# Sums of squares by column tiles in one more batch, with a newly searched order of the plan, in a fused attention and channel-mix kernel

## The chip, the cores and the metric

The kernel runs on one core of a Trainium2 chip. The metric is the device time in microseconds (us) of a whole execution. Every run of a changed kernel stands beside runs of the kernel before on the same chip, in rounds. A ratio is the mean time of one kernel's fast runs over that of the other's fast runs of the same rounds, so it is not quite the ratio of the medians that I quote beside it. A run is called slow when it lies over 1.5% above the fastest run of its kernel. The span of a profiled run is the time from its first to its last instruction. In the views, PE is TensorE, PEld its loading of weights, DVE VectorE, ACT ScalarE, POOL GpSimd and SP SyncE.

## The reference, cut to what matters

```python
kv  = einsum('bhsd,bhse->bhde', k, v)                  # 8 batches, 8 heads, 576 rows, 64 columns
out = einsum('bhsd,bhde->bhse', q, kv)
x   = out / sqrt(mean(out * out, -1) + 1e-6) * g_norm  # a sum of squares per row and head
x_prev = x shifted by one row
xk = mu_k * x + (1 - mu_k) * x_prev                    # xr the same with mu_r
k  = relu(xk @ w_k)                                    # 512 -> 1024
return sigmoid(xr @ w_r) * (k * k @ w_v)               # 1024 -> 512
```

## The kernel before

The attention works through batches 0 to 7, the channel mix through nine groups of 512 rows. Every piece of work has a name, and a list called ORDER gives the order in which the pieces are issued. Each engine executes its own pieces in that order, so a piece that waits holds up everything behind it on its engine. In the names, `q`, `k`, `v`, `u` and so on are followed by the batch or the group: `k4.2` is a product with w_k of group 4, `u6.00` an attention product of batch 6.

Three parts matter here. The first is the sum of squares. A full one multiplies by a 128-column matrix of ones and leaves the sums on all partitions. A compact one multiplies by 32 columns (`sel`), four head pairs at once, so that one inverse root suffices, and then has to spread the result over the partitions by way of DRAM:

```python
COMPACT = (5, 6, 7)
...
def ss_all(_):                                   # piece ss5: TensorE
    for i in range(2):
        for hp in range(NHP):
            nc.tensor.matmul(get(ps)[32 * hp:32 * hp + 32, i, 0:HS], sel, sq.t[:, hp, HS * i:HS * i + HS],
                             start=True, stop=True)
def rms_out(_):                                  # piece ro5: a small store, SyncE's queue
    nc.sync.dma_start(out=get(rd), in_=rc.t[0:128:16, :])
def rms_back(_):                                 # piece rb5: two broadcast loads, GpSimd's queue
    for e in range(2):
        nc.gpsimd.dma_start(out=get(rs)[64 * e:64 * e + 64],
                          in_=rd.t.rearrange("(i e) c -> e i c", e=2)[e].partition_broadcast(64))
```

The second is the way of q: from batch 3 on it is transposed by DMA from SyncE's queue, and a one-element copy on GpSimd (the gate) holds the next batch's loads back until the first transpose has landed.

```python
def q_turn(_, hs):                               # pieces qt6.0, qt6.2: SyncE's queue
    nc.sync.dma_start_transpose(out=get(qT)[:, hs].rearrange("q i (j p) -> q (i j) p", j=NJ),
                                in_=q2.t[:, hs].rearrange("p i j c -> p (i j c)"))
...
gate = add({"POOL": 0.3}, lambda _: nc.gpsimd.tensor_copy(out=turned, in_=qT.t[0:1, 0, 0:1]), ...)   # gate6
```

The third is the loads themselves: whole batches of q, k and v by GpSimd's queue, converted from fp32 to bf16 on the way, and the stores of the outputs by SyncE's queue.

## Time and profile before

| | before |
|---|---|
| median of 3 runs | 203.97 us |
| span of the profiled run | 201.7 us |
| TensorE busy | 192.6 us, 95% |
| VectorE busy | 147.2 us, 73% |
| DMA moved | 31.69 MB, 157 GB/s on average |

Each figure is a slice of 5.04 us: the busy share of TensorE and of the 16 DMA engines in tenths, and what the DMA engines moved.

```profile
PE   7999899999999999999999989999999999999991
DMA  6999999999969999999999949530742240003263
GB/s 173 200 202 207 204 205 205 204 203 248 171 100 200 217 217 193 173 207 216 207 251 248 203 70 231 156 104 5 185 143 51 66 132 15 2 0 101 69 193 108
```

TensorE has its 9s almost to the end.

### The profile page before, as it was taken

What the parts mean: (1) busy time and instruction counts of PE and PEld (TensorE: products, weight loads), DVE (VectorE), ACT (ScalarE), POOL (GpSimd) and SP (SyncE); (2) the same over time, 40 slices, a digit from 0 to 9 for tenths busy, and PEclk for the clock granted to TensorE, in tenths of its full rate; (3) what the DMA queues carried; (4) which work ended last, traced back from release to release, by engine and by line L of the source; (5) the groups of instructions that cost most, each with busy time, mean ns of one, the idle gap of its engine ahead of it and who ended that gap; (6) DMA issues with size and microseconds to landing.
All of it is one profiled execution on the core that took longest, in us unless ns stands there. A gap on an engine that the chain in (4) does not pass through costs nothing.

```text
span 201.7 us, 4116 instructions
## 1 busy us (share of the span) xinstructions
PE 192.6 (95%) x1629; PEld 103.4 (51%) x1651; DVE 147.2 (73%) x332; ACT 116.2 (58%) x148; POOL 33.4 (17%) x53
## 2 busy tenths in 40 slices
PE   7999899999999999999999989999999999999991
PEld 7867775454544454543457654444444444444451
DVE  1589988998898959799799985699486854432321
ACT  2588688666978597948723887268452226644020
POOL 7964314000050040040053010000200000000000
PEclk9999999999999999999999999999999999999998
DMA  6999999999969999999999949530742240003263
GB/s 173 200 202 207 204 205 205 204 203 248 171 100 200 217 217 193 173 207 216 207 251 248 203 70 231 156 104 5 185 143 51 66 132 15 2 0 101 69 193 108
DMA packets 39976, 31.69 MB, mean 157 GB/s; under 512 B 13812, under 2 KB 35092, under 8 KB 39956
## 3 DMA queue, kind: packets, MB, share of 16 engines
q0 software_dynamic: 21504, 18.11, 57.0%
q1 hardware_dynamic: 17780, 12.42, 25.9%
q10 hardware_dynamic: 672, 0.89, 1.3%
q8 instruction: 13, 0.21, 0.4%
q14 instruction: 7, 0.06, 0.1%
HBM read 35.33 MB, written 9.46 MB: 222 GB/s over the span
## 4 chain that ended last, share of the span: by engine, by line
PE 74%; DMA 13%; POOL 4%; ACT 3%; issue 2%; SPq 1%; DVE 0%; DVEq 0%; POOLq 0%; ACTq 0%
PE mm L795 25%; PE mm L875 24%; PE mm L853 12%; DMA w_k<-in_moe_w_k_dram 5%; DMA v<-in_v_dram 5%; DMA qT<-q 3%; PE at L649 2%; PE at L567 2%; PE mm L522 2%; PE mm L815 2%; PE mm L892 2%; PE at L892 2%; PE at L701 2%; POOL k L275 1%; POOL q L275 1%
## 5 line engine op out<-in xcount | busy, mean ns | idle before, releaser
L795 PE MATMUL mm<-xk,w_k 128*128 128x512 bf16 (+1 forms) x281 | 58.5, 355 | 0.4
L875 PE MATMUL mm<-w_v,sqk 128*128 128x512 bf16 x251 | 57.8, 379 | 0.6 <-issue 0.3
L799 ACT ACTIVATE relu<-mm 128x1024 bf16<-128x1024 f32 x36 | 36.9, 1024 | 27.1 <-PE mm L795 23.2
L795 PEld LDWEIGHTS <-w_k 128*128 128x128 bf16 x288 | 27.2, 98 | 26.7 <-issue 1.8
L875 PEld LDWEIGHTS <-sqk 128*128 128x128 bf16 x256 | 24.7, 98 | 29.2 <-issue 1.1
L853 PE MATMUL mm<-w_r,xr 128*128 128x512 bf16 x135 | 33.4, 379 | 0.8 <-issue 0.5
L879 DVE TENSOR_TENSOR out<-mm,sig 128x1024 f32<-128x1024 f32 x16 | 19.5, 1223 | 19.8 <-PE mm L875 15.8
L858 ACT ACTIVATE sig<-mm 128x1024 bf16<-128x1024 f32 x18 | 18.4, 1025 | 26.6 <-PE mm L853 26.5
L802 DVE TENSOR_TENSOR sqk<-relu 128x1024 bf16<-128x1024 bf16 x32 | 21.7, 687 | 10.9 <-ACT relu L799 10.7
L853 PEld LDWEIGHTS <-xr 128*128 128x128 bf16 x144 | 13.5, 98 | 15.6 <-issue 0.9
L185 ACT CAST uT<-at 128x576 bf16<-128x576 f32 x21 | 12.6, 641 | 12.2 <-PE at L649 12.2
L743 DVE TENSOR_SCALAR md<-d,cols 128x576 bf16<-128x576 bf16 x56 | 18.4, 371 | 0.3
L194 ACT ACT_TABLE_LOAD x12 | 15.4, 1283 | 0.2
L763 PE MATMUL mm<-zero 128*128 128x128 bf16 x137 | 12.3, 251 | 1.1 <-DVE zero L245 1.1
L717 DVE TENSOR_TENSOR xT<-uT,rs 128x1152 bf16<-128x1152 bf16 x14 | 10.5, 752 | 2.9 <-ACT rs L705 2.8
L656 DVE TENSOR_TENSOR sq<-uT 128x576 bf16<-128x576 bf16 x28 | 12.1, 451 | 0.8 <-ACT uT L185 0.6
L705 ACT ACTIVATE rs<-at,eps 128x576 bf16<-128x576 f32 x16 | 11.2, 738 | 1.8 <-PE at L701 1.7
L763 PEld LDWEIGHTS <-zero 128*128 128x128 bf16 x137 | 10.5, 116 | 2.9 <-issue 1.3
L684 POOL DMA_DIRECT2D rs<-rd x6 | 3.8, 634 | 44.2 <-DVE xk L746 20.6
L746 DVE TENSOR_TENSOR xk<-md,xT 128x1152 bf16<-128x1152 bf16 x14 | 10.6, 759 | 0.5
L746 DVE TENSOR_TENSOR xr<-md,xT 128x1152 bf16<-128x1152 bf16 x14 | 10.6, 759 | 0.5
L729 DVE TENSOR_TENSOR d<-xT 128x1152 bf16<-128x1152 bf16 x14 | 10.5, 753 | 0.2
(89 smaller groups left out, 175.2 us busy)
## 6 DMA issues: line engine op xcount, KB each, us to landing
out_dram<-out SPq DMA_DIRECT2D x22, 192.0 KB, 4.7
q<-in_q_dram POOLq DMA_DIRECT2D x6, 576.0 KB, 10.0
v<-in_v_dram POOLq DMA_DIRECT2D x6, 576.0 KB, 12.6
k<-in_k_dram POOLq DMA_DIRECT2D x6, 576.0 KB, 11.1
out_dram<-out SPq DMA_DIRECT2D x23, 128.0 KB, 2.2
rs<-rd POOLq DMA_DIRECT2D x6, 288.0 KB, 5.6
out_dram<-out SPq DMA_DIRECT2D x22, 64.0 KB, 6.6
w_k<-in_moe_w_k_dram POOLq DMA_DIRECT2D x2, 512.0 KB, 11.5
```

The lines of the kernel that those rows point to most:

```text
L185: nc.scalar.copy(out=dst, in_=src)
L194: nc.scalar.preload_act_table_set(name)
L743: nc.vector.tensor_scalar(out=get(md)[:, hp], in0=d.t[:, hp], scalar1=cols[:, m0 + hp:m0 + hp + 1], scalar2=None, op0=ALU.mult)
L746: nc.vector.tensor_tensor(out=dst[:, hs, c0:c0 + S], in0=md.t[:, hs], in1=xT.t[:, hs, 0:S], op=ALU.add)
L763: nc.tensor.matmul(get(k_ps[i])[:, 0, 0:128], zero[:, 0:128], zero[:, 128:256], start=not k_seen[i], stop=not k_seen[i])
L795: nc.tensor.matmul(get(ps)[:, fc % 2, a0:a1], w_k_sb[:, cc, 128 * fc:128 * fc + 128], xk[:, cc, x0:x0 + a1 - a0], start=(cc == 0), stop=(c ...
L799: nc.scalar.activation(out=get(rt), in_=ps.t, func=AF.Relu)
L802: nc.vector.tensor_mul(out=get(sqk)[:, 2 * f2:2 * f2 + 2, :], in0=rt.t, in1=rt.t)
L853: nc.tensor.matmul(get(ps)[:, ci % 2, :], xr[:, cc, n0:n0 + 128], w_r_sb[:, cc, :], start=(cc == 0), stop=(cc == NHP - 1))
L858: nc.scalar.activation(out=get(sg), in_=ps.t, func=AF.Sigmoid)
L875: nc.tensor.matmul(get(ps)[:, ci % 2, :], sqk.t[:, fc, 128 * ci:128 * ci + 128], w_v_sb[:, fc, :], start=(fc == 0), stop=(fc == NFC - 1))
L879: nc.vector.tensor_mul(out=get(ot)[:, xs, :], in0=ps.t[:, xs, :], in1=sg.t[:, xs, :])
```

## The change

Its intent: the compact sums, which are cheaper on TensorE and on ScalarE, in batch 4 as well, and an order searched anew so that the pieces fit. The diff has one line outside the list, and nearly the whole list is new. Its core, with cuts marked by dots:

```diff
-    COMPACT = (5, 6, 7)
+    COMPACT = (4, 5, 6, 7)
 ORDER, around batches 4 to 6:
-... ss4.10 ... ss4.00 ... rr4.10 ... ss4.11 ... rr4.00 rr4.11 mul4.2 ... ss4.01 rr4.01 mul4.0 ...
+... qt5.0 ss4 ... rr4 ro4 ... qt5.2 ... gate5 loadq6.0 ... rb4 mul4.0 mul4.2 d4.0 d4.2 ... loadk6.0 loadv6.0 ...
-... k4.4 qt6.0 qt6.2 ... u6.10 u6.01 ... rb5 mul5.0 ... u6.00 ... gate6 loadk7.0 ...
+... qt6.0 u6.00 ... u6.01 ... rb5 mul5.2 ... k4.4 k4.5 ... qt6.2 u6.11 u6.10 ... gate6 loadq7.0 ...
 ORDER, start:
-setup loadq0.2 ident ... w_k0 idle:3 k0.a0.1 ... w_k1 idle:6 k0.a1.3 ...
+setup loadq0.2 loadk0.2 loadv0.2 loadq0.6 ... ident ... w_k1 idle:8 k0.a1.2 ... w_k0 ... idle:3 k0.a0.2 ...
```

## The prediction

> **What bounds the kernel now.** I read the page first, then the chain that ended last, then TensorE's timeline and busy times by stretch, then the ScalarE and GpSimd timelines around the few waits. The busy line and the chain's shares:
>
> ```profile
> PE 192.6 (95%) x1629; PEld 103.4 (51%) x1651; DVE 147.2 (73%) x332; ACT 116.2 (58%) x148; POOL 33.4 (17%) x53
> PE 74%; DMA 13%; POOL 4%; ACT 3%; issue 2%; SPq 1%; DVE 0%; DVEq 0%; POOLq 0%; ACTq 0%
> ```
>
> 95% alone is no proof, since 137 fillers (L763, multiplications by zero) are in it. The chain, in order of time, tells what is real:
>
> ```profile
> 9.83 10.92 DMA w_k<-in_moe_w_k_dram
> 20.75 0.05 issue
> 20.80 1.49 PE mm L522 x12
> ...
> 95.52 0.39 PE at L671 x8
> ...
> 138.80 3.45 PE mm L875 x16
> ...
> 195.80 1.76 PE at L892 x16
> ```
>
> There are three parts. (1) Up to 20.80 us the channel mix waits for the first half of w_k: GpSimd issued it at 9.83, behind twelve q, k, v loads, and it landed at 20.75 while the queue moved 200 to 208 GB/s. (2) From 20.80 to 197.56 (195.80 + 1.76) TensorE works. The busy times by stretch leave about 2.5 us idle in those 176.8 (10.00 minus 9.75, 9.64, 9.95 ... in the ten-microsecond stretches). (3) From 197.56 to the span's end at 201.7 lie the last product, store and closing: 4.1 us. The measured time, 203.97, is 2.3 above the span.
>
> So in the middle only work taken off TensorE, or an idle gap closed, counts. The gaps I can name:
>
> ```profile
> 20.80 1.49 PE L522 MATMUL mm<-xk,w_k 128*128 128x256 bf16 x12 [0.59 <-DMA w_k<-in_moe_w_k_dram]
> ...
> 56.88 1.02 PE L875 MATMUL mm<-w_v,sqk 128*128 128x512 bf16 x4 [0.15 <-ACT sig L858]
> ...
> 116.46 0.95 PE L567 MATMUL at<-v,k 96*64 96x64 bf16 x48 [0.53 <-DMA v<-in_v_dram]
> ```
>
> The first lies in part 1; the other two are 0.68 us together. Most of the rest is pieces of 0.05 and 0.16 marked "issue", which any order will have.
>
> **What the Trainium skill says.** "TensorEngine Tiling (Array Packing)", section Tiling Modes: a 128x32 configuration has four column tiles that can work in parallel, and changing the mode drains the engine. The trace agrees on both: eight compact sums (sel, 32 columns) take 0.39 and 0.36 us in the chain, while two full ones (ones, 128 columns) take 0.24 to 0.25, so eight would take 0.98; the speedup is 2.6, not 4. "ScalarE: Activation LUTs", section What ACT_TABLE_LOAD costs, gives about 1283 ns for a load plus 1380 ns of drain. The trace has twelve L194 loads of 1283 ns, but no such drain: the load at 54.51 ends at 55.79 and the sigmoid starts at 55.81. I charge 1.28. "DMA: Bandwidth & Descriptors", section Issuing engines are not separate DMA queues, has it that loads from all queues share the same 16 engines; the flat 200 to 208 GB/s of the start fits. A new order of the same bytes therefore does not bring w_k much earlier.
>
> **The change part by part.** There are two parts.
>
> *Compact sums in batch 4.* Removed: four groups of two 128x288 multiplications by ones (4 x 0.245 = 0.98 us TensorE) and four inverse roots (4 x 738 ns = 2.95 us ScalarE). Added: eight by sel (0.37 us), one inverse root (740 ns), a small store and two broadcast loads (2 x 635 ns on GpSimd, 0.59 MB). TensorE saves **0.61 us**, which counts fully because it lies in part 2. ScalarE saves 2.2 us, which by itself counts nothing at 58%. Price: the way through DRAM. In batch 5 the sums start at 95.52, the root ends at 96.68, the loads go out at 101.83 after a wait for the small store and land about 5.6 later, so about 12 us in all. The new plan has batch 4's sums some 13 us of TensorE work (adding its pieces up) before batch 4's product on VectorE, and 24 before k4.4, the first reader. So it should be hidden, if barely on VectorE.
>
> *The new order.* Instruction counts per engine hardly change otherwise; fillers go from 137 to 132.
>
> Start: the twelve loads ahead of w_k are the same bytes, but the making of ident no longer stands behind the first GpSimd load (the second load went out at 2.39 after a start at 1.30 with 0.76 for the first). It moves after the fifth load. The early queue fills 0.3 to 0.4 us sooner, and as bandwidth limits, w_k should land sooner by about that: **-0.3**. The halves of w_k swap, which alone changes nothing. VectorE's work before the first xk is of the same size (13 to 14 us of durations in both). After the first w_k matmul only 3 fillers remain instead of 6 (each 0.057): **-0.17**.
>
> Middle: closing the two named gaps would give -0.68. I count half, **-0.3**, because the new order shortens leads elsewhere. Adding durations up to each reader on both engines: k2.6 comes 0.5 us of VectorE work after xk2.2, where the first k2 reader had 3 to 8; k3.6 has 0.9 after xk3.0 instead of 11; k5.6 has 0.9 after xk5.0 instead of 18. These leads overstate VectorE's need, since its instructions overlap by some 10% (durations add to 164 us, busy is 147), so most will just fit. The tightest ScalarE place is at about 94 to 105 us, before batch 6's u: a root (0.74), q relays moved from VectorE (1.02 + 1.02 + 0.83), sig3.0 (1.28 table + 1.03), **two table loads in a row** from the piece "table", which now stands between two sigmoids and so loads the root's set only to have it replaced (2 x 1.28), sig3.1 (1.03) and the kv copy (0.37): 9.9 us for 10 to 11 us of TensorE work. A late q load would show there as a TensorE wait. The total of table loads stays twelve plus the initial one, so without that stray piece it would have been ten. I allow **+0.5** for this and the short leads together, and **+0.2** at v0.2.1: it comes about 0.6 us earlier against the second half of w_v, which landed at 35.0.
>
> Tail: the last six multiplications' worth of pieces are the same and ordered the same, and the second r8 pair moves forward, which only permutes TensorE work: **0**.
>
> Sum: -0.61 - 0.3 - 0.17 - 0.3 + 0.5 + 0.2 = -0.7. A plan kept after a new search is more likely to fit its leads than my additions can tell, so I go to -1.1: **202.9 us**.
>
> **The rivals.**
>
> *A: nothing is lost in the new order.* All named gaps vanish and no new ones come: -0.61 - 0.4 - 0.17 - 0.68 = -1.9, so 202.1. For it: the order was searched. Against it: the old order was too, and leaves only 2.5 us. This also gives a floor: taking all 2.5 us would end at about 200.3, which a stream of "issue" pieces excludes. A gain above 2% (below 199.9) would need TensorE work to vanish that the diff does not remove, or w_k to land 3 us earlier at the same bandwidth.
>
> *B: the relay through DRAM and the in-order queues take the saving back.* Batch 4's broadcast load now stands in GpSimd's queue behind the gate that waits for batch 5's transposed q, and the small store stands behind those transposes in SyncE's queue. VectorE is in order too, so its product of batch 4 stops everything behind it, ksq and out included. For it, before:
>
> ```profile
> 101.83 1.26 POOL L684 DMA_DIRECT2D rs<-rd  x2 [10.89 <-DMA rd<-rc]
> 104.16 0.60 POOL L612 COPY turned<-qT 1x1 bf16<-1x1 bf16 x1 [1.07 <-DMA qT<-q]
> ```
>
> The broadcast and the gate do queue in one another's way there. Against: VectorE still had slack around that time (1.0 us idle before the product at 100.64). If it hits, TensorE waits 1 to 3 us between 95 and 115: 204 to 206.
>
> *C: the start gets worse.* VectorE is full from 15 to 25 us (4.96 to 5.00 of 5.00), so a badly placed piece delays the first xk directly. For it: that stretch was reordered most. Against it: xk0.2 and xk0.3 now come first and w_k1 needs just those. It would add 0.5 to 1: about 203.7.
>
> **Range and chances.** The certain gain is 0.6; start and gaps are worth at most 1.3 more, and new waits would cost 0 to 2. From A to a mild B gives 201.5 to 204.5. A gain over 2% needs 4.1 us, more than all idle time plus the saving: 4%. A loss over 2% needs several new waits at once: 2%.
>
> **What would show it.** Right: eight more short L671 and eight fewer L701 multiplications, L705 down from sixteen instructions to twelve; first L522 at about 20.4; two L194 next to each other near 100 us; TensorE busy 9.8 or more in all stretches from 30 to 190; the last multiplication ending near 196.5. Wrong: TensorE waits over 0.5 us put down to xk or uT between 55 and 120 (B), or a first L522 after 21 (C); a gain over 2 us would mean that I overlooked idle time inside TensorE's busy time.

## The result, and the profile after

The changed kernel took 212.65 us (median of 4 runs, 212.26 to 216.06) beside 204.18 of the kernel before. The ratio of the fast runs is 1.0417 (95% interval 1.0375 to 1.046): 4.2% slower, and far outside the predicted range.

The profiled run has a span of 210.5 us, 8.8 more than before. Its page has, of the parts shown of before, the busy line, the rows by slice (now 5.26 us each) and the granted clock:

```profile
PE 197.2 (94%) x1646; PEld 103.6 (49%) x1646; DVE 148.4 (70%) x328; ACT 115.1 (55%) x149; POOL 36.0 (17%) x55
...
PE   7979999999999999999674999999999999999992
...
PEclk9999999999999999999996699999999999999999
DMA  6999999999999999899999999334650006400445
```

TensorE's row has a hole, 6 7 4, between 100 and 116 us, and at its end and behind it two slices of low clock. The DMA row has its 9s as before, now up to 131 us, but for one 8. What TensorE waited for from 25 us on (columns: total us, times, longest):

```profile
PE at L649 <- DMA qT<-q: 4.2, 1, 4.2
PE mm L875 <- DVE out L879: 1.5, 1, 1.5
PE at L892 <- DVE out L899: 0.5, 1, 0.5
```

In the kernel before, the longest wait in that stretch was the 0.53 us for batch 6's v. The chain of what ended last shows the new one. First the stretch of the kernel before, then of the changed one (start, us, what):

```profile
98.66 0.03 issue
98.69 5.35 DMA qT<-q
104.04 0.02 issue
```

```profile
96.50 0.75 ACT rc L676
...
98.98 14.36 DMA qT<-q
113.33 0.04 issue
113.38 0.70 PE at L649 x8
```

Batch 6's first transpose goes out at nearly the same time in both (98.69 and 98.98). It lands after 5.35 us in one and after 14.36 in the other. Nothing stands ahead of it in SyncE's queue that was not there before; the transfer itself is slow. The last columns of the stretches from 100 to 115 us say how (columns: stretch, its length, busy time and count of TensorE, weight loads, VectorE, ScalarE, GpSimd, then granted clock, DMA busy share, GB/s), before and after:

```profile
100.00:105.00 5.00, 5.00 (x35) 2.22 (x35) 4.29 (x9) 1.23 (x2) 1.86 (x3) 1.00 1.28 256
105.00:110.00 5.00, 4.83 (x86) 3.77 (x80) 4.54 (x10) 1.53 (x2) 2.34 (x3) 1.00 1.02 244
110.00:115.00 5.00, 4.95 (x43) 3.34 (x43) 4.89 (x12) 3.51 (x6) 0.00 (x0) 1.00 1.31 202
```

```profile
100.00:105.00 5.00, 3.27 (x16) 1.34 (x14) 4.80 (x9) 4.96 (x7) 1.27 (x2) 1.00 1.26 222
105.00:110.00 5.00, 4.13 (x63) 2.10 (x62) 4.87 (x11) 1.57 (x3) 0.00 (x0) 1.00 1.17 134
110.00:115.00 5.00, 1.62 (x13) 0.91 (x13) 1.00 (x2) 1.12 (x2) 1.14 (x3) 0.72 1.25 91
```

The share is the time of all packets over the engines' time, so that one above 1 means that packets overlap on an engine. In the changed kernel the DMA engines are as busy, but from 105 us on they move only 134 and then 91 GB/s. The 244 and 202 before are mostly plain loads and stores and no fair comparison. The stretch in which the transposes ran before is one, 100 to 105 us: 256 GB/s at a share of 1.28.

The records of single packets in the two traces tell what ran beside what. Before, the 2304 packets of batch 6's two transposes (256 bytes each) ran from 101.7 to 104.5 us, 1017 of them in the microsecond from 103 in which they were alone, and batch 5's broadcast began with its packets at 104.4. In the changed kernel they ran from 103.1 to 117.5 us: 119 to 492 in each microsecond from 103 to 106, beside v's load, and 7 to 188 in each from 107 to 115, beside the broadcast (issued at 102.48, landed up to 14.7 us later). The broadcast's packets of 4608 bytes slowed as well, from 312 ns on average to 668.

What came between is on GpSimd's queue, before and after (start, us, engine, line, operation):

```profile
88.64 0.78 POOL L275 DMA_DIRECT2D q<-in_q_dram  x1 [1.08 <-ACT relu L799]
89.41 0.77 POOL L275 DMA_DIRECT2D k<-in_k_dram  x1
90.17 0.77 POOL L275 DMA_DIRECT2D v<-in_v_dram  x1
```

```profile
87.65 0.92 POOL L275 DMA_DIRECT2D q<-in_q_dram  x1 [1.08 <-DVE out L879]
88.56 1.27 POOL L684 DMA_DIRECT2D rs<-rd  x2
89.81 0.82 POOL L275 DMA_DIRECT2D k<-in_k_dram  x1
90.59 0.81 POOL L275 DMA_DIRECT2D v<-in_v_dram  x1
```

Batch 4's broadcast, `rs<-rd`, is the new line. With it k and v land at 103.0 and 107.2 instead of 99.2 and 102.8. Before, the last packet of v's load began 0.5 us after the transposes' first one; now the two run beside each other for 3.7 us, and so the transposes are still under way when the broadcast starts.

The last product ends at 206.97 instead of 197.56, 9.4 us later. Of that I can name: 1.0 by the first product of group 1 (43.32 against 42.30), 1.5 and 4.2 and 0.5 for the three waits, and about 2.4 for the 32 products of group 4 behind the long wait, which take 6.10 us at a low clock. Less 0.61 for the cheaper sums and 0.5 for the wait for v that is gone, this makes 8.5. About 1 us is spread over gaps that I do not name. Between the last product and the end of the span lie 3.5 us instead of 4.1.

### The profile page after: what moved, and what is told of

The parts are those of the page before. It is cut to its first block, busy times and chain, and to the rows that moved or that the text cites. A ratio compares the mean times of both kernels' runs of the same rounds, so it can differ in the third digit from the quotient of the medians.

```text
span 210.5 us, 4132 instructions
## 1 busy us (share of the span) xinstructions
PE 197.2 (94%) x1646; PEld 103.6 (49%) x1646; DVE 148.4 (70%) x328; ACT 115.1 (55%) x149; POOL 36.0 (17%) x55
## 4 chain that ended last, share of the span: by engine, by line
PE 84%; DMA 7%; DVE 5%; ACT 2%; SPq 1%; issue 0%; ACTq 0%
PE mm L795 28%; PE mm L875 23%; PE mm L853 14%; DMA qT<-q 7%; PE mm L763 3%; PE at L649 2%; PE at L567 2%; PE at L892 2%; PE mm L815 2%; PE mm L892 2%; PE at L701 1%; PE mm L522 1%; DVE xT L432 1%; PE at L627 1%; DVE xk L478 1%; PE at L671 1%
## 5 line engine op out<-in xcount | busy, mean ns | idle before, releaser
L795 PE MATMUL mm<-xk,w_k 128*128 128x512 bf16 (+1 forms) x288 | 61.6, 367 | 0.0
L875 PE MATMUL mm<-w_v,sqk 128*128 128x512 bf16 x256 | 58.4, 379 | 1.5 <-DVE out L879 1.5
L795 PEld LDWEIGHTS <-w_k 128*128 128x128 bf16 x288 | 28.4, 102 | 27.7 <-issue 2.0
L853 PE MATMUL mm<-w_r,xr 128*128 128x512 bf16 x144 | 34.3, 379 | 0.2 <-ACT sig L858 0.2
L879 DVE TENSOR_TENSOR out<-mm,sig 128x1024 f32<-128x1024 f32 x16 | 19.6, 1223 | 16.1 <-PE mm L875 10.6
L743 DVE TENSOR_SCALAR md<-d,cols 128x576 bf16<-128x576 bf16 x56 | 18.3, 369 | 0.3
L185 ACT CAST uT<-at 128x576 bf16<-128x576 f32 x18 | 11.0, 640 | 10.7 <-PE at L649 10.7
L194 ACT ACT_TABLE_LOAD x12 | 15.4, 1283 | 0.2
L763 PE MATMUL mm<-zero 128*128 128x128 bf16 x132 | 12.2, 255 | 1.1 <-DVE zero L245 1.1
L612 POOL COPY turned<-qT 1x1 bf16<-1x1 bf16 x4 | 2.4, 604 | 55.2 <-DMA qT<-q 55.2
L684 POOL DMA_DIRECT2D rs<-rd x8 | 5.0, 633 | 39.5 <-DMA rd<-rc 18.3
L763 PEld LDWEIGHTS <-zero 128*128 128x128 bf16 x132 | 10.4, 118 | 1.9 <-DVE zero L245 1.1
## 6 DMA issues: line engine op xcount, KB each, us to landing
v<-in_v_dram POOLq DMA_DIRECT2D x6, 576.0 KB, 14.9
k<-in_k_dram POOLq DMA_DIRECT2D x6, 576.0 KB, 12.4
```

What stands on the lines that cost most here:

```text
L194: nc.scalar.preload_act_table_set(name)
L743: nc.vector.tensor_scalar(out=get(md)[:, hp], in0=d.t[:, hp], scalar1=cols[:, m0 + hp:m0 + hp + 1], scalar2=None, op0=ALU.mult)
L763: nc.tensor.matmul(get(k_ps[i])[:, 0, 0:128], zero[:, 0:128], zero[:, 128:256], start=not k_seen[i], stop=not k_seen[i])
L795: nc.tensor.matmul(get(ps)[:, fc % 2, a0:a1], w_k_sb[:, cc, 128 * fc:128 * fc + 128], xk[:, cc, x0:x0 + a1 - a0], start=(cc == 0), stop=(c ...
L853: nc.tensor.matmul(get(ps)[:, ci % 2, :], xr[:, cc, n0:n0 + 128], w_r_sb[:, cc, :], start=(cc == 0), stop=(cc == NHP - 1))
L875: nc.tensor.matmul(get(ps)[:, ci % 2, :], sqk.t[:, fc, 128 * ci:128 * ci + 128], w_v_sb[:, fc, :], start=(fc == 0), stop=(fc == NFC - 1))
```

## The experiments

My theory after the traces was that the DMA engines are the cause: batch 4's broadcast, 0.59 MB where they are full, pushes the loads into the transposes and those into batch 5's broadcast. The rivals were the new order (its short leads, its start, its table loads) and the queues' order alone. Piece names are those of ORDER. All 18 kernels gave correct results. Where my theory forecast a loss, it was often larger than expected: e6, e9, e15 and e16 lie above their ranges, and so do e3, by 0.3 us, and e5, by 0.1.

### The waits of the changed kernel, one at a time

**e1_gate_first.** The gate that waits for batch 6's first transpose goes ahead of batch 5's broadcast on GpSimd, so that the two do not meet.

```diff
-... rb5 mul5.2 ... gate6 loadq7.0 ...
+... gate6 rb5 mul5.2 ... loadq7.0 ...
```

> Edit: in the changed kernel, GpSimd's gate of batch 6 (the tiny copy that waits for the first transposed q of batch 6) is moved ahead of batch 5's two broadcast loads, so these loads start only when that transpose has landed. Nothing else moves. Theory 1 (collision): the transpose of batch 6 took 14.4 us instead of 5.4 because it shared the DMA engines with batch 5's broadcast loads; then it should land by about 107 to 108 us, TensorE's 4.2 us wait before batch 6's u and the low clock after it (2.6 us) should go, and the time should fall from 212.4 to 205 to 207. Theory 2 (queueing: batch 6's k and v loads, pushed back by batch 4's extra 0.59 MB, hold the transpose up): the broadcast plays no part, the transpose still lands after 111 us, and the time stays above 211.

210.14 us, ratio 1.0318 (1.0274 to 1.0363). The transposes took 8.9 us, and TensorE waited for none. But the wait moved on to batch 5's x, whose broadcast now began at 109.0:

```profile
121.54 3.21 PE L795 MATMUL mm<-xk,w_k 128*128 128x512 bf16 x8 [2.38 <-DVE xk L746]
```

So keeping the two apart does quicken the transposes. Of the 9.0 us that the first one lost in the changed kernel, the meeting with the broadcast makes 5.5 by this run (14.4 against 8.9), and the rest, in which the loads ran beside it, 3.5 (8.9 against 5.35). The time was a miss, because the delay is passed on rather than removed.

**e2_u6_late.** Batch 6's first two attention products go behind four pieces of group 4, so that TensorE need not wait for the transpose.

```diff
-... qt6.0 u6.00 uc6.00 u6.01 uc6.01 rb5 ... k4.0 k4.1 relu4.0 qt6.2 ...
+... qt6.0 rb5 ... k4.0 k4.1 relu4.0 u6.00 uc6.00 u6.01 uc6.01 qt6.2 ...
```

> Edit: in the changed kernel, batch 6's first two u products (and their evictions) are placed behind four of group 4's k products instead of ahead of them. DMA is untouched. If what matters is only that TensorE's in-order queue has a late product at its head, the transpose still takes about 14 us, but TensorE works 3.45 us of it off: the wait should fall from 4.2 to about 0.8 us, the low clock should go, and the time should be 206 to 208. If another wait stands right behind it (a reader of batch 4's or 5's x), the time stays above 210.

212.92 us, ratio 1.0455: no gain, a miss. The first pair no longer waited, but the second transpose was late as well, and TensorE waited 4.4 us for that one. So the place of the waiting pieces alone is not the cause.

**e4_table_early.** The stray table load of ScalarE goes to the start, where the kernel before had it.

```diff
-... kv0.0 kvc0.0 ... ql6.3 ql6.2 table r3.2 ...
+... kv0.0 kvc0.0 table ... ql6.3 ql6.2 r3.2 ...
```

> Edit: the one stray load of the root's table is moved from between two sigmoids of group 3 to the start, into an idle stretch of ScalarE, as before. This removes the 1.28 us load that stands just ahead of the first inverse root at 12.44 us and one pair of loads at 102.6. Theory: the start of the changed kernel is bound by ScalarE and VectorE, not by w_k; the first k product, at 21.29 us, should start at 20.1 to 20.6 and the time fall by 0.6 to 1.3 us (211.1 to 211.8). The pair at 102.6 us should count nothing, as ScalarE then waits for TensorE. Rival (the pair delays batch 6): the wait of 4.2 us shrinks by 1 us or more and the time falls by over 2 us.

211.73 us, ratio 1.030 (1.0193 to 1.0407), with a widely spread set of runs and a profile that fell in the slow state. The first product with w_k began at 20.99 instead of 21.29, and the second lot of them at 22.60, behind VectorE's xk as before. That is less than the 20.1 to 20.6 expected. The transposes were still waited for, 5.4 us. So in this slow profile the first product came 0.3 us sooner, which by the next ones was gone, and the pair of loads in the middle is not the cause.

### The change taken apart

**e3_no_compact4** and **e5_order_alone.** The new order with full sums in batch 4. In e3 their pieces stand in one block, in e5 they are spread between products of group 2, and one output's eviction goes behind the last products.

```diff
-    COMPACT = (4, 5, 6, 7)
+    COMPACT = (5, 6, 7)
-... ss4 ... rr4 ro4 v2.2.0 v2.2.1 v2.3.0 v2.3.1 ... rb4 mul4.0 ...
+e5: ... ss4.00 rr4.00 v2.2.0 ss4.01 rr4.01 v2.2.1 ss4.10 rr4.10 v2.3.0 ss4.11 rr4.11 v2.3.1 ... mul4.0 ...
```

> Edit: the new order is kept, but batch 4's sums are full again (four full groups with four inverse roots where the compact one stood, no trip through DRAM). This adds 0.6 us to TensorE and takes 0.59 MB of broadcast away. Theory 2 (queueing): k and v of batch 6 land about 3 to 4 us earlier (v by about 104 instead of 107.2), the transpose follows, and the loss shrinks to under 3 us: 205 to 208. VectorE's 2.0 us wait for batch 4's factors and TensorE's 1.5 us wait for the output product should go in any case. Theory 1 alone (collision with batch 5's broadcast, which then would start right behind the earlier loads): the transpose still overlaps it and takes over 10 us; 209 to 212.

> Edit: the new order without the compact sums in batch 4, as in the last run, but the four full sums are spread between group 2's products so that TensorE doesn't wait 2.1 us for an inverse root (that wait was made by my placing them in a block), and the very last eviction is moved behind the products it held up (0.5 us). If the new order alone is sound and the trip through DRAM is what it cannot bear, this should be within 1.5 us of the kernel before: 203 to 205.5, with the transpose of batch 6 landing within 4 to 7 us and no TensorE wait over 1 us after 30 us. If the order itself loses much, it stays above 206.

e3 took 208.27 us (ratio 1.0205, 1.0133 to 1.0278, unclear), 2.3 us of it waits that my block of pieces made. e5 took 205.6 us, ratio 1.0083 (1.0041 to 1.0125). In both the first transpose of batch 6 landed in 3.9 to 6.4 us and TensorE waited for neither. The new order without the compact sums costs 0.8%, about 1.7 us; without the moved eviction, which removes a wait of 0.5 us, it might be a little more. In e5's profile the largest wait after the start is 1.5 us for an x of group 4.

**e6_compact_alone** and **e16_compact_clean.** The old order with compact sums in batch 4. In e6 the small store `ro4` stood ahead of batch 5's transposes, which made them land 2.4 us late (the gate behind them ran at 89.78 instead of 87.39), a fault that the changed kernel has not; e16 mends it.

```diff
-    COMPACT = (5, 6, 7)
+    COMPACT = (4, 5, 6, 7)
-... rr4.00 rr4.11 mul4.2 ... ksq3.0 ... qt5.2 ... ss5 loadq6.0 ... ss4.01 rr4.01 mul4.0 d4.0 ...
+e6:  ... ss4 rr4 ro4 ... qt5.0 gate5 ... qt5.2 ... ss5 loadq6.0 rb4 ... mul4.0 mul4.2 d4.0 d4.2 ...
+e16: ... ss4 rr4 ... qt5.0 gate5 ... qt5.2 ro4 ... ss5 loadq6.0 rb4 ... mul4.0 mul4.2 d4.0 d4.2 ...
```

> Edit: the old order with batch 4's sums compact, nothing else: sums, root and small store where the third full sum stood, the broadcast behind batch 6's q load (where the new order has it), batch 4's products, differences and the first mix moved together behind it. Theory: the 0.59 MB ahead of k and v of batch 6 push these back by 3 to 4 us (v lands at about 106 instead of 102.8), the transposes of batch 6 then share the engines with them and with batch 5's broadcast and take 9 us or more instead of 5.4. In the old order TensorE has 3.5 us of work between the landing and its use, so it waits less: 205 to 209. Rival (the trip is hidden in the old order and only the new order exposes it): 203.2 to 203.8, i.e. the 0.6 us of TensorE work saved.

> Old order, batch 4 compact, with its small store to DRAM behind batch 5's second transpose instead of ahead of the first (the run of the old order with batch 4 compact had it ahead, which sent batch 5's transposes out 2.4 us later). Theory 1 (0.59 MB more where the DMA engines are full): batch 5's transposes go out as in the kernel before, but k and v of batch 6 still land about 3 us later, and batch 6's transposes still meet batch 5's broadcast: 208 to 211.5. Rival (the small store's place in SyncE's queue was the cause in that run): 203.5 to 205.

e6 took 211.51 us (ratio 1.0381, 1.034 to 1.0422), e16 213.54 (1.0446, 1.0399 to 1.0493). The fault was not the cause; without it the time was no better. The chain and TensorE's timeline of e16:

```profile
100.42 14.26 DMA qT<-q
...
114.72 0.69 PE L648 MATMUL at<-qT,kv 64*64 64x288 bf16 x8 [5.88 <-DMA qT<-q]
```

That is the wait of the changed kernel, in the old order (which needs the second of batch 6's two transposes first, the new order the first). The compact sums of batch 4, with the pieces of batch 4 that move behind them, bring the whole loss by themselves: 4.5% here and 0.8% for the order in e5, against 4.2% for both together, so the two do not add up.

### The traffic alone

These four are the kernel before, full sums in batch 4 and all, with a load added whose result nobody reads. The broadcast ones copy the form and size of `rb4` (0.59 MB).

```diff
 e9:  ... ss5 loadq6.0
+     dum                                  # two broadcast loads
      ql6.2 ...
 e8:  ... loadk6.0 loadv6.0
+     dum                                  # the same, behind v
 e13: ... ss5 loadq6.0
+     dum                                  # nc.gpsimd.dma_start(out=dum, in_=part("q", 0, 0, H - 1)): plain, 0.52 MB
 e10: ... mul6.0 qt7.2
+     dum                                  # two broadcast loads, at 122.8 us
```

> Edit: the same two additional loads, but issued right behind q of batch 6 and ahead of its k and v, which is where the changed kernel has batch 4's broadcast. Theory: k and v of batch 6 land 3 to 4 us later (103 and 106), and batch 5's own broadcast, which stands behind them, meets the transposes: these take 9 us or more though nothing of the new order is here. If so, the time rises to 205 to 209 as in the run with the compact sums alone. If the transposes stay under 7 us, the place in the queue isn't what matters.

> Edit: the old kernel with two additional broadcast loads of the same form (64 partitions x 4 rows of 576, from a DRAM tile of zeros to a tile that nobody reads), issued right behind v of batch 6, so that they run while batch 6's q is transposed. All else is as before; v of batch 6 should land at 102.8 as before. Collision theory: the transposes take 9 to 14 us instead of 5.4, and each 256 B packet about 0.1 instead of 0.02 engine-us. Rival (only bandwidth counts): 0.59 MB at 200 GB/s is 3 us, so 5.4 becomes at most 8 us.

> The kernel before with one plain dummy load between batch 6's q and k loads, where the dummy broadcast stood: seven of the eight heads of batch 0's q again (0.52 MB written, packets of the size of the other q, k and v loads). Theory 1 (room on the DMA engines is what is short): as bad as the broadcast there, 210 to 216, v landing over 15 us after its issue. Theory 2 (it is the broadcast's form, packets of 4608 bytes that hold up the transposes' packets of 256): under 206, transposes in under 7 us.

> The kernel before with the same two dummy broadcast loads (0.59 MB) as in the two runs before, but issued behind batch 7's second transpose, at about 125 to 135 us, where the DMA share of the kernel before falls from over 0.9 to 0.2. Theory 1 (the DMA engines are full until about 116 us, and anything added there pushes back what stands behind it): within 0.5% of before, 203.5 to 205.0, and the dummy loads land in under 7 us. Theory 2 (broadcast loads cost by themselves, wherever they stand, by GpSimd's issuing or by disturbing VectorE): 207 to 213 as at the earlier places.

The awaited transpose is the second of batch 6, as in e16.

| run | median, us | ratio (95%) | awaited transpose, us | TensorE waited for it, us |
|---|---|---|---|---|
| e9, broadcast ahead of k and v | 215.76 | 1.0574 (1.0525 to 1.0623) | 17.8 | 7.4 |
| e8, broadcast behind v | 211.98 | none | 16.1 | 9.2 |
| e13, plain load ahead of k and v | 215.12 | 1.0543 (1.0486 to 1.0601) | 17.0 | 8.6 |
| e10, broadcast at 122.8 us | 203.74 | 0.9987 (0.9957 to 1.0016) | 8.3 | 1.4 |

e8 fell three times in four above 210 us and once at 205.24, so by the rule three of its runs are slow, its profile too, and it gets no ratio; I build nothing on it. It also missed its expectation for v (15.3 us, not 12.6). The others are plain. The same broadcast costs 12.0 us at 89 us and nothing at 123 us, just before the DMA row falls (the added load landed in 7.4 us there; under 7 was expected). In e10 the second transpose took 8.3 us and TensorE waited 1.4 for it before the added load was even issued, so the old order by itself is not free of such waits. A plain load of the same weight, in the ordinary packets of the q, k and v loads, costs nearly as much, 10.8 us. So neither the sums, nor VectorE's wait for them, nor the form of the added load is needed: added bytes in the full stretch are enough. Two things stay in all of these runs: batch 5's own broadcast, and, in e9 and e13, the added load's place ahead of k and v in GpSimd's queue. e14 and e15 below take them away. In e13 a wait of 8.6 us stood where the kernel before had none:

```profile
117.76 0.69 PE L649 MATMUL at<-qT,kv 64*64 64x288 bf16 x8 [8.63 <-DMA qT<-q]
```

### Where the broadcasts stand

**e15_rb4_behind_v6** and **e14_four_not_five.** Both start from e16. e15 puts batch 4's broadcast behind k and v; e14 makes batch 5's sums full, so that only one broadcast runs before 110 us, as in the kernel before.

```diff
 e15:
-... ss5 loadq6.0 rb4 ... loadk6.0 loadv6.0 r3.2 ...
+... ss5 loadq6.0 loadk6.0 loadv6.0 rb4 ... r3.2 ...
 e14:
-    COMPACT = (4, 5, 6, 7)
+    COMPACT = (4, 6, 7)
-... ss5 ... rr5 ro5 store2.1 r3.1 ... sig3.0 v3.0.0 v3.0.1 v3.1.0 ... rb5 mul5.0 ...
+... ss5.00 rr5.00 ... store2.1 r3.1 ss5.01 rr5.01 ... v3.0.0 ss5.10 rr5.10 v3.0.1 ss5.11 rr5.11 sig3.0 v3.1.0 ... mul5.0 ...
```

> As the run with the small store mended, with batch 4's broadcast behind batch 6's k and v loads in GpSimd's queue, so that they no longer stand behind it. If the order of the loads is what costs: v lands in under 14 us and the time is 203.5 to 206. If it is room on the DMA engines: the v wait goes, but the broadcast lands about 10 us after its issue, batch 4's x comes late and TensorE waits for it or for the output of group 3 before it, 207 to 212.

> As the run with the small store mended, but batch 5 goes back to full sums: as much broadcast before 110 us as in the kernel before, only one batch earlier. If the meeting of batch 5's broadcast with batch 6's transposes is the main cost: the transposes land in under 7 us and the time is 203.5 to 206. If the delay of batch 6's k and v by the broadcast ahead of them is the main cost: TensorE still waits 2 to 4 us for v, 206 to 209.

e15 took 214.66 us, ratio 1.0546 (1.0494 to 1.0597). k and v no longer stood behind the broadcast, but v still took 15.8 us (12.6 before), and the broadcast took 16.18 us to land, VectorE stood before its product with it, and TensorE waited for an output behind that:

```profile
PE mm L874 <- DVE out L878: 10.2, 1, 10.2
```

So the queue's order decides who waits, not whether somebody does. e14 took 205.64 us, ratio 1.0075 (1.0039 to 1.0111): with one broadcast in that stretch the transposes were not waited for, although v needed 16.6 us behind the broadcast and TensorE waited 0.8 for it. The first transpose took 9.3 us (issued at 99.67, the gate behind it at 108.95), where under 7 was expected; that is close to e1's 8.9, again without a broadcast beside it. Another 2.5 us are waits for ScalarE, which I put down to my placing of the roots. What does not fit is the second broadcast.

### Room made elsewhere

Three output tiles of groups 2 and 3 (1.57 MB) are stored later, for which the output buffers go from three to four. In e11 and e12 all three go behind batch 7's first transpose, in e18 and e19 two of them behind its second. e12 and e18 have full sums in batch 4; e11 is e6 with this, e19 is e16 with it.

```diff
-        "out": (3, (128, 2, C), FP32),
+        "out": (4, (128, 2, C), FP32),
-... store2.1#2 store1.1#2 store2.0 store1.1 rr5 ro5 store2.1 ... store3.0#2 store2.0#2 ... qt7.0 store3.0 ... qt7.2 ...
+e11, e12: ... store1.1#2 store1.1 rr5 ro5 ... qt7.0 store2.1#2 store2.1 store2.0#2 store2.0 store3.0#2 store3.0 ... qt7.2 ...
+e18, e19: ... store1.1#2 store1.1 rr5 ro5 ... qt7.0 store2.1#2 store2.1 ... qt7.2 store2.0#2 store2.0 store3.0#2 store3.0 ...
```

> The kernel before with the same three output tiles' stores put off and four output buffers, nothing else. Theory 1: the wait of 0.53 us for batch 6's v goes, v lands in under 12 us, and the time is 203 to 204.5. Theory 2: no change, 204, v still at 12.6. If putting off stores makes a wait for an output buffer, TensorE or VectorE will show it near the last output of group 4 and the time will be 205 or more.

> The old order with batch 4 compact (which ran at 211.5), and with three output tiles' stores (of groups 2 and 3, 1.57 MB) put off from about 88 to 108 us until behind batch 7's first transpose, with four output buffers in place of three. Theory 1 (room on the DMA engines): the v wait of 3.7 us and the long transposes go, 203 to 206. Theory 2 (queue order: k and v of batch 6 simply stand behind the broadcast in GpSimd's queue, and stores go by another queue): 209.5 to 212.

> The kernel before with the stores of groups 2 and 3 put off as in the earlier run (206.5), but those of two of the three output tiles behind batch 7's second transpose instead of ahead of it, where they held it up by 3.2 us. If the wait of 3.2 us was all that was lost: TensorE has no wait over 0.5 us between 90 and 140, 202.5 to 203.8, a little faster than before. If another transfer meets the late stores: 204.5 or more.

> Batch 4 compact in the old order without the fault in SyncE's queue (213.5), and the late stores that gave 202.75 alone. If the stores' 1.57 MB were room enough for the 0.59 MB of the broadcast: 202 to 204.5. If what counts is that two broadcasts, the transposes and the loads of batch 6 meet between 98 and 112 us, and the stores taken away lay mostly before that: 208 to 213.

e12 took 206.5 us (ratio 1.0118): the wait for v went and TensorE was busy without a gap up to 130 us, as expected, but then it waited 3.2 us for batch 7's second transpose, which stood behind the late stores. e18 takes that away: 202.75 us, ratio 0.9943 (0.9915 to 0.997), 0.6% faster than the kernel before, a small gain but clear of the noise. In the stretch from 30 to 190 us TensorE was busy 157.64 of 160 us before, and here:

```profile
30.00:190.00 160.00, 159.06 (x1220) 76.56 (x1219) 122.24 (x245) 95.29 (x111) 16.86 (x25) 1.00 0.82 151
```

e11 took 217.5 us (ratio 1.0644), 6 us more than e6, and missed badly. It carries e6's fault and e12's, but e12's shows as a wait of 0.75 us only; the awaited transpose of batch 6 took 17.1 us and TensorE waited 6.4 for it. Why the late stores made e6 worse is not shown, and it speaks against room alone as the measure. e19, free of both faults, took 209.59 us (ratio 1.0266, 1.0209 to 1.0323) against 213.54 of e16. So the stores' room gives about 4 of the 9 us back, and not the rest: the awaited transpose still took 12.4 us. The stores taken away lay largely before the meeting, and the meeting of transposes and broadcast remains.

### The low clock

**e21_fillers_in_wait.** The changed kernel with 80 multiplications by zero ahead of `u6.00`, where TensorE waits for the transpose.

```diff
 def u_mm(_, gp=gp, cs=cs, ps=ps):
+    for _ in range(80 if b == 6 and gp == 0 and cs.start == 0 else 0):
+        nc.tensor.matmul(get(ps)[:, 0, 0:128], zero[:, 0:128], zero[:, 128:256], start=True, stop=True)
     for x in range(2):
```

> The changed kernel with 80 multiplications by zero (about 0.057 us each, 4.5 us) put ahead of batch 6's first attention product, where TensorE waits 4.2 us for the transpose. If the low granted clock comes from the idle wait: the clock in 110 to 120 us is 0.95 or more, the 32 products of group 4 behind it take 3.5 us instead of 6.1, and the time is 209.5 to 211. If it comes from something else: the products take 6 us all the same, and the time is 212 to 213.5.

212.76 us, ratio 1.0439: the time did not move, a miss. The mechanism did show. First the timeline of the changed kernel, then of this one:

```profile
114.00 6.10 PE L795 MATMUL mm<-xk,w_k 128*128 128x256 bf16 x32
```

```profile
110.13 4.63 PE L647 MATMUL at<-zero 128*128 128x128 bf16 x80
...
115.06 3.67 PE L797 MATMUL mm<-xk,w_k 128*128 128x256 bf16 x32
```

The granted clock was 1.00 in 110 to 120 us (in the changed kernel 0.50 from 112.2 to 119.0), and the same 32 products took 3.67 us instead of 6.10. In the profiled run TensorE was 1.2 us later than in the other before the wait (105.69 against 104.49 at the same products; 0.6 of it dates from the start, where this execution had a clock of 0.50 from 14.9 to 18.3 us and the other had not), and after the products it had a gap of 1.08 us that the profile puts down to nothing. So 2.4 us is what the low clock costs the products; what it costs the kernel this run leaves open.

## Why the prediction was wrong

The prediction said 202.9 us in a range of 201.5 to 204.5, and gave slower by over 2% a chance of 2 in 100. It was wrong in direction. By its own steps:

- **What bounds the kernel.** Right for TensorE, and incomplete: I quoted the 200 to 208 GB/s for the start only and never read the DMA row beyond it. The row has its 9s up to 116 us but for one slice. An estimate: the loads convert fp32 to bf16, and one that the profile counts as 576 KB reads 1152 KB (8 x 576 x 64 x 4 bytes), so 205 GB/s written is some 410 read, close to the 425 that the Trainium skill, "DMA: Bandwidth & Descriptors", section Measured (HBM→SBUF, 128 partitions, SWDGE, issued from GpSimd), gives as measured for a load of 16 MB. By this estimate there was hardly room; no run here shows the limit itself.
- **The compact sums save 0.61 us of TensorE.** Right as a term, and the sums take 0.36 to 0.39 us here too.
- **"So it should be hidden, if barely on VectorE."** This is the step that failed. I priced the way through DRAM as a latency against a lead, 12 us against 13, and counted the 0.59 MB as nothing. At the 205 GB/s of that stretch, 0.59 MB are 2.9 us of all DMA engines. k and v landed 3.8 and 4.4 us later, which is somewhat more. This laid the loads beside the transposes (3.5 of the 9.0 us, by e1) and the transposes beside batch 5's broadcast (the other 5.5), where the engines moved 91 to 134 GB/s. e16 shows that this term alone makes 4.5%; e9 and e13 that the traffic makes it without any sums; e10 that it is free at 123 us; e14 that one broadcast fits there and two do not. I had cited the skill's statement that all queues share the 16 engines, from the section Issuing engines are not separate DMA queues, and used it only for w_k. These runs agree with it: a load from GpSimd's queue delayed a transpose from SyncE's by 9 us.
- **The start, -0.3 and -0.17.** w_k's first half landed at about 20.1 instead of 20.75, sooner than predicted, although it was issued no earlier (9.89 against 9.83). But the first product with it began at 21.29 instead of 20.80, because VectorE's xk came later. This is rival C, with its sign (a first L522 after 21) and its size, 1.0 us by group 1. The fillers saved nothing visible (12.2 us against 12.3 of L763).
- **The gaps, -0.3, and the short leads, +0.5.** e5 puts the whole new order, start included, at 0.8%, about 1.7 us, where I had -0.07 for it (-0.3 - 0.17 - 0.3 + 0.5 + 0.2). The two table loads side by side did occur, at 102.61, and cost nothing that e4 could show.
- **The trust in a searched order, -0.4.** Not borne out: the search's plan is slower than the old one in e5 too.
- **Rival B.** It named the right part, the relay through DRAM, and the right place, 95 to 115 us, and its waits of 1 to 3 us were 4.2 and 1.5. But it looked for the fault in queues and in VectorE's order. Its sign, waits put down to xk or uT, did not come: TensorE waited for qT itself and for an output. Its counterargument, VectorE's slack, says nothing of the DMA engines. The low clock behind a long wait was in no rival. The Trainium skill has it: "TensorE: Matmul & The Clock Gate", Part 1, says that after an idle window of about 3.4 us the clock is halved, and comes back after as long a busy one. The trace agrees on the half: a wait of 4.2 us, and a granted clock of 0.50 from 112.2 to 119.0 us. The way back took 5.6 us of work here, and on how idle TensorE must be the traces differ (last section).

What stays open: how transposes and broadcasts beside each other get so slow. By the trace's records of single packets, the 256-byte packets of batch 6's transposes took 22 ns on average before and 48 after, and far fewer of them ran in a microsecond, but why is not shown by any run. Nor did any run put the added bytes on a queue other than GpSimd's. About 1 us of the loss is unnamed.

## What to carry to other kernels

Before you move work from a compute engine to a transfer, read the DMA row over the whole span, not at the start alone: a transfer has a latency, which a lead can hide, and a weight, which only free DMA time can. Where the engines are full, ask what the added bytes will push into what; here 2.9 us of extra traffic became about 9. The same reading tells where to gain: moving 1.57 MB of stores from where the DMA engines were full to where they had room made the kernel before 0.6% faster.

## What the Trainium skill lacked or had wrong

- "DMA: Bandwidth & Descriptors" has a bandwidth for a DMA transpose by itself, and says that all queues share the engines, but has no figure for the speed of a transpose beside other loads. Here the engines moved 91 GB/s at a busy share of 1.25 with transposes beside a broadcast, against 256 at 1.28 in the transposes' stretch of the kernel before, and the first transpose took 14.36 us instead of 5.35.
- "TensorE: Matmul & The Clock Gate", Part 1, has the half clock come after at least one idle window of about 3.4 us. Here less was enough: in e1 a wait of 2.4 us (119.2 to 121.5) was followed by a clock of 0.50 from 122.0 to 125.4, while a wait of 3.2 us in e12 was followed by none.
- "ScalarE: Activation LUTs", section What ACT_TABLE_LOAD costs, adds a drain of 1380 ns to each load. The traces don't show it: in the kernel before, each of the twelve loads of 1283 ns begins within 0.02 us of the end of the activation before it, and where the next activation was ready, that began 0.01 us after the load.
- "TensorEngine Tiling (Array Packing)", section Tiling Modes, has four column tiles in parallel; no page has a measured gain for four column tiles alone. Eight sums of this form went 2.6 times as fast as full ones (0.37 us against an estimated 0.98).
